# Folding two more modulation vectors onto 64 partitions in a linear-attention and token-mixer block

## The chip, the cores and the metric

The kernel runs on one core of a Trainium2 chip. The metric is device microseconds of one execution, median over runs. The engines are TensorE (PE, its weight loads as PEld), VectorE (DVE), ScalarE (ACT), GpSimd (POOL) and SyncE (SP, which issues most DMAs). Each executes its own instructions in program order, and they wait for each other by semaphores.

## The reference

With x of 2048 tokens by 448 channels (float32), 16 heads of 28 channels:

```python
mod = (silu(c) @ w_mod).reshape(1, 6, 1, 448)
sa, ca, ga, sb, cb, gb = mod[:, 0], ..., mod[:, 5]
h = layernorm(x) * (1 + ca) + sa
x = x + ga * linear_attention(h, wqkv, wo)      # phi(q) (phi(k)^T v) / (phi(q) sum phi(k))
h = layernorm(x) * (1 + cb) + sb
x = x + gb * token_mlp(layernorm(h), w1, b1, w2, b2)   # gelu MLP across the 2048 tokens
```

The six modulation vectors are numbered 0 to 5 here and in the code: 0 and 1 are sa and ca of the attention, 2 is ga, 3 is sb, 4 is cb (1 + cb is stored), 5 is gb. The change concerns vectors 3 and 4, the fourth and fifth.

## The kernel before

Tokens come in 16 tiles of 128. A value in float32 that TensorE is to multiply exactly is cut into a high part (rounded to TensorE's float32r) and a low part (the rest), and a product is taken as two or three float32r matmuls. The program is scheduled by hand: what an engine does, and in which order, is the order in which the code issues it.

**Modulation vectors 2 to 5.** The rows of w_mod for vector j come as four tiles `wm{j}_{k}` of 112 partitions. `mod_part(j, k)` multiplies tile k with silu(c) and adds it into `acc{j}` (112 x 448) on VectorE. Then `mod_split(j)` prepares `acc` for TensorE, and `mod_sum2(j)` sums over the partitions with a matmul whose weights are all ones, so that the sum stands on all 128 partitions; `mod_out` copies it out of PSUM on ScalarE. `mod_split` has two ways:

```python
    def mod_split(j):
        acc = macc.pop(j)
        if j in FOLDED:
            both, low = halves(acc, slot, f"mh{j}")
            low()
            macc[j] = (both,)
        else:
            macc[j] = (moving(slot, f"mh{j}", parts=G), moving(slot, f"ml{j}", parts=G))
            split(acc, *macc[j])
```

- Not folded: `split` (lines 84 and 85) makes the high part `mh` by a copy on ScalarE and the low part `ml` by a subtraction on VectorE, each 112 x 448 in a buffer of its own, and `mod_sum2` (line 260) issues two matmuls.
- Folded: `halves` adds partitions 64 to 111 of `acc` to partitions 0 to 47 (VectorE, line 238), copies the 64 partitions that remain to partitions 0 to 63 of one buffer on ScalarE (line 240: the high part), and `low` writes the difference to partitions 64 to 127 of the same buffer (VectorE, line 243). `mod_sum2` then issues one matmul over 128 partitions.

**Stage 1** is a loop over the tiles t = 4 to 15 (tiles 0 to 3 are begun ahead of it): project k, its exponential and relu, the normalized tokens `xn` cut into `xh` and `xl`, phi(k) cut into `pkh` and `pkl`, and their outer products, which add into four PSUM banks `cacc` (`a_outer`, line 551) four tiles later. Each tile ends with odd jobs: `mod_part` of vector 4 at t = 9 to 12 (by `MOD_AT`), of vector 3 at t = 13 and 14, `mod_split(2)` at t = 11, the multiplication of a tile of `wo` with vector 2 from t = 13, and loads of `pr`, pieces of w1, by SyncE (`load_to`, line 316). The exponentials of q for the next tile (`eq`, `rq`, lines 468 and 469) are issued at the start of the next tile.

**The tail of stage 1.** Behind the loop stand, in the order of issue: the last `pk` parts; the sum of all phi(k), cut into `zh` and `zl`; the outer products of tiles 12 to 15; the last `wo` and the last two `mod_part` of vector 3; `split_to(2)`, which cuts two pieces of w1 (`ph` on ScalarE, `pl` on VectorE); the `zp` matmuls and their copy `zb`; `mod_split(4)`, `mod_split(3)`; `split_to(4)`; two q projections; the four `cs` (line 795 on ScalarE, 796 on VectorE); `split_to(6)`; `mod_sum2(4)`; the `kvb` matmuls (line 805), which read `cs`; `mod_sum2(3)`. From `kvb` come `kvm`, the `wp` matmuls and the weights `Wph`, `Wpl` of the output projection.

**Stage 2** is a loop over the tiles for the output projection, the two layer norms (which use vectors 4 and 3) and the first MLP product; stage 3 is the rest of the MLP. Nothing in them is edited.

**Buffers.** Tiles of SBUF made with `slot` share a pool of 74 buffers. A tile takes a free one, and its first writer, be it an engine or a DMA, waits until the last reader of the buffer's former tile is done.

Of the kernel before, what the change touches and what calls it, by code (L numbers as in the profile page):

```python
# [41 lines left out]
WARM = 6  # L42
POOL_LOW = (0, 2)
PRE = 9
FOLDED = (2, 5,)
MID = 5
NSLOT, NTOK = 74, 27
LOAD2, SPLIT2 = 12, 4
# [4 lines left out]
def block_kernel(ctx: ExitStack, tc: tile.TileContext, x, xt, wqkv, wo, w1, b1, w2, b2, c, wmod, wfirst, out):  # L53
# [23 lines left out]
    def moving(new, name, dt=F32R, parts=P):  # L77
        return new(name, dt=dt, parts=parts, w=512)[:, 16:16 + D]
# [4 lines left out]
    def split(full, hi, lo):  # L83
        nc.scalar.activation(hi, full, AF.Copy)  # L84
        nc.vector.tensor_sub(lo, full, hi.bitcast(F32))  # L85
# [150 lines left out]
    def halves(acc, new, name):  # L236
        n = acc.shape[0] - 64
        nc.vector.tensor_add(acc[:n], acc[:n], acc[64:])
        both = moving(new, name)
        nc.scalar.activation(both[:64], acc[:64], AF.Copy)  # L240

        def low():
            nc.vector.tensor_sub(both[64:], acc[:64], both[:64].bitcast(F32))
        return both, low
# [11 lines that stand above are left out]
    def mod_sum2(j):  # L256
        ps = bank(f"modp{j}")
        part = macc.pop(j)
        for i, m in enumerate(part):
            nc.tensor.matmul(ps[:, :D], ones_r[:m.shape[0], :], m, start=(i == 0), stop=(i == len(part) - 1))  # L260
        return ps
# [11 lines left out]
    def w_low(j, ch):  # L273
        w, r = Whi[j, ch], raw_w[j, ch]
        p = slice(0, P) if ch < 3 else slice(64, P)
        if ch < 3:
            Wlo[j, ch] = moving(tslot, f"wl{j}_{ch}")
        out = Wlo[j, ch] if ch < 3 else w[p]
        nc.vector.scalar_tensor_tensor(out, r[p], col[1][p, ch:ch + 1], w[p].bitcast(F32),
                                       op0=ALU.mult, op1=ALU.subtract)  # L280

    def row_part(j, ch):
        if ch == 0:
            accb[j] = slot(f"accb{j}")
            nc.vector.tensor_scalar_mul(accb[j], raw_w[j, 0], col[0][:, 0:1])
        else:
            nc.vector.scalar_tensor_tensor(accb[j], raw_w[j, ch], col[0][:, ch:ch + 1], accb[j],
                                           op0=ALU.mult, op1=ALU.add)

    def row_sum(j):  # L290
        rowb[j] = bank(f"rowb{j}")
        ws = [Whi[j, ch] for ch in range(4)] + [Wlo[j, ch] for ch in range(3)]
        for i, w in enumerate(ws):
            nc.tensor.matmul(rowb[j][:ROWS, :D], sel_s, w, start=(i == 0), stop=False)

    def row_bias(j):
        nc.tensor.matmul(rowb[j][:ROWS, :D], sel_b, accb.pop(j), start=False, stop=True)
# [82 lines left out]
    def a_stats_dve(ts):  # L380
        g, ve = a_group(ts)

        b6 = {}

        def first(i):
            b6[i] = small.tile([P, 6], F32, name=f"st{ts[i]}", tag="st")
            nc.vector.bn_stats(b6[i], X[ts[i]])

        def second(i):
            nc.vector.bn_aggr(mv[ts[i]][:, 0:2], b6[i])  # L390

        def end():
            nc.vector.tensor_scalar_add(ve, g[:, :, 1:2].to_broadcast([P, len(ts), 2]), EPS)
            a_pow(g, ve)
            groups[ts[0]] = g
        return first, second, end
# [11 lines left out]
    def a_transpose(t):  # L408
        ps = bank(f"rw{t}")
        tps[t], tps[t + 1] = ps[:ROWS - 64, :P], ps[64:ROWS, :P]  # L410
        nc.tensor.transpose(ps[:ROWS, :P], rowst[t // 2 % RING][:, :ROWS].bitcast(F32), ident)
# [29 lines left out]
    def project(t, j, name):  # L441
        projects([(t, kind, ch) for ch in range(3) for kind in ("hh", "wl", "hl")] + [(t, "hh", 3)], j, name)

    def close(t, j):
        ps = pps.pop((t, j))
        nc.tensor.matmul(ps[:, :D], heads[t][1][:ROWS, 384:], Wrow[j][:ROWS], start=False, stop=True)  # L446
        return ps[:, :D]
# [31 lines left out]
    def a_q(t):  # L479
        project(t, 0, "qp")  # L480
        qps[t] = close(t, 0)
        del heads[t]
# [5 lines left out]
    def a_phi_q(keep=0):  # L488
        a_exp_q(keep)
        for t in sorted(eqs):  # L490
            pq[t] = phi_q(t)
# [50 lines left out]
    def a_outer(t):  # L542
        if not cacc:
            cacc.extend(bank(f"cacc{ch}") for ch in range(4))
        xh, xl = xss.pop(t)
        kh, kl = pks.pop(t)
        for ch in range(4):
            s = slice(ch * P, (ch + 1) * P)
            todo = [(xh, kh), (xh, kl)] + ([(xl, kh)] if ch < 3 else [])
            for i, (a, b) in enumerate(todo[::1 if t > 1 else 2]):  # L550
                nc.tensor.matmul(cacc[ch][:, :D], a[:, s], b, start=(t == 0 and i == 0),  # L551
                                 stop=(t == NT - 1 and i == len(todo) - 1))
        if t < 2:
            for ch in range(4):
                nc.tensor.matmul(cacc[ch][:, :D], xh[:, ch * P:(ch + 1) * P], kl, start=False, stop=False)
# [118 lines left out]
    for t in range(4, NT):  # L674
        if 5 < t < NT - 1:
            project(t + 1, 1, "kp")
        kp = close(t, 1) if t > 4 else kps[4]
        if t == 9:
            row_sum(0)
            row_bias(0)  # L680
        if t > 4:
            a_outer(t - KV_LAG)
        if t % 2 and 4 < t < NT - 2:
            a_transpose(t + 1)
        if t in Q_EARLY:
            a_q(Q_EARLY[t])
        if t == 12:
            mp = mod_sum2(2)
        pair = t % 2 and 7 < t + 3 < NT
        if pair:  # L690
            first, second, end = a_stats_dve((t + 3, t + 4))
            first(0)
        if 5 <= t < 9:
            w_low(0, t - 5)
        if pair:
            second(0)
        if 5 <= t < 9:
            row_part(0, t - 5)
        a_phi_q(t in Q_EARLY)
        if t == 9:  # L700
            a_exp(t, kp)
        if t % 2 and 4 < t < NT - 2:
            a_copy(t + 1)
            a_copy(t + 2)
        if t != 9:
            a_exp(t, kp)
        if 7 < t + 3 < NT:
            a_split_high(t + 3)
        a_pk_parts(t - 1)
        highs = HIGH_AT.get(t, (t - 2,))  # L710
        for i in highs[:1]:
            a_norm(i)
            a_high(i)
        if t % 2 == 0 and 4 < t < NT - 3:
            low = a_rows(t + 2)
        a_pk(t, kp)
        if t % 2 == 0 and 4 < t < NT - 3:
            low()
        if 7 < t + 3 < NT:
            a_split_low(t + 3)  # L720
        for i in highs[1:]:
            a_norm(i)
            a_high(i)
        if pair:
            first(1)
        for i in highs:
            a_low(i)
        if pair:
            second(1)
            end()  # L730
        sum_end()
        if 4 <= t < 8:
            w_high(0, t - 4)
            if t == 7:
                w_row(0)
        if t == 9:
            row_out(0)
        if t == 12:
            mod_out(2, mp)
            make_mask()  # L740
        if t in FETCH:
            load_xt(FETCH[t])
            load_x(FETCH[t])
        if 7 <= t < 11:
            mod_part(2, t - 7)
        if t == 11:
            mod_split(2)
        for j, i in MOD_AT.get(t, ()):
            mod_part(j, i)
        if t in (7, 10):  # L750
            load_mod(4 if t == 7 else 3)
        if t == 10:
            load_qkv(2, tslot)
        if t == 8:
            for g in range(4):
                w = tslot(f"wo{g}", parts=G)
                nc.sync.dma_start(w, wo[g * G:(g + 1) * G, :])
                wo_sb.append(w)
            b1c = cst.tile([P, NF], F32, name="b1c")
            nc.sync.dma_start(b1c, b1)  # L760
            b2c = cst.tile([P, NT], F32, name="b2c")
            nc.sync.dma_start(b2c, b2)
        if t >= 13:
            nc.vector.tensor_mul(wo_sb[t - 13], wo_sb[t - 13], mods[2][:G])
        load_to(PRE_LOAD.get(t, 0))
# [18 lines left out]
        nc.tensor.matmul(zp[:, :D], ones_r, pk, start=(i == 0), stop=(i == 1))  # L784
    zb = tslot("zb")
    nc.scalar.activation(zb, zp[:, :D], AF.Copy, bias=S * 1e-6)
    mod_split(4)
    mod_split(3)
    load_to(14)
    split_to(4)  # L790
# [184 lines left out]
    for i in range(NT + LAG):  # L975
# [15 lines left out]
        t = i - LAG  # L991
# [277 lines left out]
    for o0, n in W1G[1:]:  # L1269
# [5 lines left out]
        for r in range(first, NT):  # L1275
# [5 lines left out]
            if xleft:  # L1281
                t = xleft.pop(0)
# [81 lines left out]
```

## Time and profile before

| | |
|---|---|
| median of 3 runs | 436.17 us (435.62 to 436.36) |
| profiled execution | 435.4 us, span 433.7 us |
| PE busy | 428.1 us (99%), 2333 matmuls |
| DVE busy | 362.2 us (84%), 813 instructions |
| ACT busy | 278.5 us (64%), 595 instructions |
| POOL busy | 119.6 us (28%) |
| chain that ended last | PE 92%, DVE 4%, DMA 2% |

Times in the profile count from the start of the span, and lines (L260) are those of the kernel's code. A row of the timeline has the start, the duration, engine, line, operation, output and inputs by the program's names, shape and count; behind it, in brackets, how long the engine was idle just before and what it waited for. Rows that follow each other and are alike are merged ("x2"). Durations of pipelined instructions overlap, so that the distance from start to start, not the duration, is what an instruction costs its engine's queue.

### The profile page before, as it was taken

The numbers are of one execution on the slowest core, as the hardware profiler recorded it, in microseconds if no ns is written. First come the engines' busy times: TensorE is split into PE (matmuls) and PEld (weight loads), VectorE is DVE, ScalarE is ACT, GpSimd is POOL, SyncE is SP. The second block draws the span as 40 slices with busy tenths as digits, with TensorE's granted clock in tenths as the row PEclk, the third lists the DMA queues.
The fourth block names the chain that finished last, engine by engine and source line by source line (L and its number), as shares of the span: only waits on it lengthen the run. The fifth ranks groups of instructions, "written<-read, shape, count | busy, mean of one in ns | idle before, by whom it ended". The sixth has DMA issues, their size and how long they took to land.

```text
span 433.7 us, 7208 instructions
## 1 busy us (share of the span) xinstructions
PE 428.1 (99%) x2333; PEld 395.5 (91%) x2333; DVE 362.2 (84%) x813; ACT 278.5 (64%) x595; POOL 119.6 (28%) x198
## 2 busy tenths in 40 slices
PE   8999999999999999999999999999999999999996
PEld 7788899999899989989999999999999999999996
DVE  4999987689799999996579695739799998898893
ACT  5899868658578799985855263537464664645550
POOL 2336444300025577775200000010113131122010
PEclk9999999999999999999999999999999999999999
DMA  8998996574200036345427461587479977886430
GB/s 278 384 334 179 242 249 152 107 225 164 86 1 0 26 73 148 73 98 121 147 85 241 144 212 50 167 209 201 85 181 215 228 157 153 218 176 125 82 54 32
DMA packets 63941, 66.14 MB, mean 152 GB/s; under 512 B 4960, under 2 KB 55456, under 8 KB 63904
## 3 DMA queue, kind: packets, MB, share of 16 engines
q1 hardware_dynamic: 54832, 50.90, 37.8%
q0 software_dynamic: 8784, 14.32, 21.1%
q10 hardware_dynamic: 288, 0.46, 0.5%
q8 instruction: 18, 0.29, 0.3%
q14 instruction: 19, 0.16, 0.1%
HBM read 46.30 MB, written 7.34 MB: 124 GB/s over the span
## 4 chain that ended last, share of the span: by engine, by line
PE 92%; DVE 4%; DMA 2%; issue 0%; POOL 0%; ACT 0%; SPq 0%; DVEq 0%
PE y L1159 19%; PE up L939 10%; PE up L938 10%; PE up L940 10%; PE y L1160 9%; PE cacc L551 8%; PE qp L439 7%; PE op L881 6%; PE kp L439 5%; PE tq L851 1%; PE op L888 1%; DMA wr<-in_qkv_dram 1%; DMA xt<-in_xt_dram 1%; PE qp L446 1%; PE kvb L805 1%; PE wp L955 1%
## 5 line engine op out<-in xcount | busy, mean ns | idle before, releaser
L939 PE MATMUL up<-h2l,ph 128*128 128x448 f32 x224 | 81.3, 363 | 0.0
L938 PE MATMUL up<-h2h,ph 128*128 128x448 f32 x224 | 81.2, 362 | 0.0
L940 PE MATMUL up<-h2h,pl 128*128 128x448 f32 x224 | 80.8, 361 | 0.0
L1114 POOL DMA_DIRECT2D a<-a x16 | 14.2, 962 | 137.8 <-DMA a<-in_B_w_dram 77.6
L938 PEld LDWEIGHTS up<-h2h,ph 128*128 128x128 f32 x224 | 42.0, 188 | 3.2
L940 PEld LDWEIGHTS up<-h2h,pl 128*128 128x128 f32 x224 | 41.9, 187 | 3.0
L939 PEld LDWEIGHTS up<-h2l,ph 128*128 128x128 f32 x224 | 42.0, 188 | 2.6 <-DVE h2l L935 0.3
L85 DVE TENSOR_TENSOR pl<-pr,ph 128x512 fp32r<-128x512 f32 x46 | 30.8, 688 | 4.1 <-ACT ph L84 3.3
L1165 ACT ACTIVATE cc<-y 128x448 f32<-128x448 f32 x24 | 13.0, 546 | 26.8 <-PE y L1160 26.8
L84 ACT ACTIVATE ph<-pr 128x512 fp32r<-128x512 f32 x46 | 27.6, 623 | 0.8 <-PE up L940 0.5
L1078 DVE TENSOR_TENSOR u<-u,mod 128x448 f32<-128x448 f32 x14 | 8.7, 623 | 21.7 <-ACT u L1077 21.5
L1077 ACT ACTIVATE u<-up,b1c 128x448 f32<-128x448 f32 x14 | 8.8, 625 | 24.1 <-PE up L940 23.5
L1179 POOL DMA_DIRECT2D out_dram<-yt x14 | 12.7, 908 | 40.8 <-DVE yt L1170 31.4
L439 PE MATMUL kp<-wh,hh 128*128 128x448 f32 x64 | 23.7, 375 | 0.0
L551 PE MATMUL cacc<-pkh,xh 128*128 128x448 f32 x64 | 23.6, 369 | 0.0
L439 PE MATMUL qp<-wh,hh 128*128 128x448 f32 x64 | 23.4, 366 | 0.0
L831 POOL TENSOR_SCALAR den<-den 128x16 f32<-128x16 f32 x16 | 8.8, 549 | 45.4 <-DVE den L828 45.4
L551 PE MATMUL cacc<-pkl,xh 128*128 128x448 f32 x56 | 20.3, 362 | 0.0
L881 PE MATMUL op<-wph,pth 128*128 128x448 f32 x48 | 18.7, 390 | 0.0
L1120 DVE TENSOR_TENSOR a<-a,s 128x512 f32<-128x512 f32 (+1 forms) x32 | 18.5, 622 | 0.0
L84 ACT ACTIVATE s2h<-s 128x512 fp32r<-128x512 f32 (+1 forms) x16 | 8.3, 569 | 15.5 <-DVE s L1120 15.5
L1159 PE MATMUL y<-ub,a11h 128*128 128x448 f32 x56 | 18.2, 375 | 0.0
(239 smaller groups left out, 1378.1 us busy)
## 6 DMA issues: line engine op xcount, KB each, us to landing
pr<-in_B_w_dram SPq DMA_DIRECT2D x56, 256.0 KB, 3.1
a<-in_B_w_dram SPq DMA_DIRECT2D x32, 256.0 KB, 4.4
a<-in_B_w_dram SPq DMA_DIRECT2D x32, 192.0 KB, 4.2
xt<-in_xt_dram SPq DMA_DIRECT2D x16, 256.0 KB, 5.0
x<-in_A_x_dram SPq DMA_DIRECT2D x16, 224.0 KB, 5.0
wm<-in_B_wmod_dram SPq DMA_DIRECT2D x16, 196.0 KB, 5.4
out_dram<-x SPq DMA_DIRECT2D x14, 224.0 KB, 2.2
out_dram<-yt POOLq DMA_DIRECT2D x14, 224.0 KB, 5.7
```

The lines of the kernel that those rows point to most:

```text
L84: nc.scalar.activation(hi, full, AF.Copy)
L85: nc.vector.tensor_sub(lo, full, hi.bitcast(F32))
L439: nc.tensor.matmul(pps[t, j][:, :D], a[:, ch * P:(ch + 1) * P], w, start=first, stop=False)
L551: nc.tensor.matmul(cacc[ch][:, :D], a[:, s], b, start=(t == 0 and i == 0), stop=(t == NT - 1 and i == len(todo) - 1))
L881: nc.tensor.matmul(opb[t][:, :D], a, b, start=(ch == n == 0), stop=False)
L938: nc.tensor.matmul(ps[:, :D], hi[:, sl], mh, start=first, stop=False)
L939: nc.tensor.matmul(ps[:, :D], hi[:, sl], ml, start=False, stop=False)
L940: nc.tensor.matmul(ps[:, :D], lo[:, sl], mh, start=False, stop=last)
L1114: nc.gpsimd.dma_start(w, a, accum_op=ALU.add)
L1120: nc.vector.tensor_tensor(w, raw2[q, a][i], raw2[q, b][i], op=op)
L1159: nc.tensor.matmul(ps[:, :D], h[:, s], w, start=opens and r == 0, stop=False, skip_group_check=True)
L1160: nc.tensor.matmul(ps[:, :HD], l[:, s], wh, start=False, stop=closes and r == PAIRS - 1, skip_group_check=True)
```

## The change

Vectors 3 and 4 join 2 and 5 in `FOLDED`, so that `mod_split` takes the folded way for them and `mod_sum2` issues one matmul each. `mod_split(4)`, which stood behind the copy `zb` in the tail, is issued in the loop instead, at t = 14, ahead of that tile's `mod_part(3, 1)`. `mod_split(3)` stays in the tail.

```diff
-FOLDED = (2, 5,)
+FOLDED = (2, 3, 4, 5)
...
         if t == 11:
             mod_split(2)
+        if t == 14:
+            mod_split(4)
         for j, i in MOD_AT.get(t, ()):
             mod_part(j, i)
...
     nc.scalar.activation(zb, zp[:, :D], AF.Copy, bias=S * 1e-6)
-    mod_split(4)
     mod_split(3)
     load_to(14)
     split_to(4)
```

## Prediction

> **What bounds the kernel now.** I read the engine totals first, then the chain of work that ended last, then the waits of TensorE, and last the timeline of each engine around the two places where the diff edits. Totals and chain of the page:
>
> ```profile
> PE 428.1 (99%) x2333; PEld 395.5 (91%) x2333; DVE 362.2 (84%) x813; ACT 278.5 (64%) x595; POOL 119.6 (28%) x198
> ...
> PE 92%; DVE 4%; DMA 2%; issue 0%; POOL 0%; ACT 0%; SPq 0%; DVEq 0%
> ```
>
> TensorE is busy for 99% of the span and is 92% of the chain. It executes in program order and there is hardly an idle stretch behind its start, so a matmul that goes saves its time, and any stall that comes is paid in full: no later wait is large enough to take it back. The question is therefore only what VectorE (DVE) and ScalarE (ACT) hand to TensorE late. One stage of the windows view, and the one wait of a weight load in this region (waits of PEld):
>
> ```profile
> core 0: us, PE busy (x) PEld busy (x) DVE busy (x) ACT busy (x) POOL busy (x), PEclk, DMA share, GB/s
> 97.80:102.80 5.00, 5.00 (x26) 4.52 (x25) 4.96 (x10) 4.58 (x10) 0.00 (x0) 1.00 0.53 188
> PEld kvb L805 <- DVE cs L796: 0.2, 1, 0.2
> ```
>
> From 97.8 to 102.8 us VectorE is busy for 4.96 of 5.00 us, and what stands at the end of that stretch, the four `cs` operations, is what the `kvb` matmuls wait for. TensorE reaches `kvb` just as the first `cs` ends: cover there is zero, though TensorE loses nothing yet. TensorE in that region, from its timeline:
>
> ```profile
> 93.62 0.36 PE L551 MATMUL cacc<-pkh,xl 128*128 128x448 f32 x1
> ...
> 97.82 0.36 PE L784 MATMUL zp<-zl,ones_r 128*128 128x448 f32 x1
> ...
> 102.43 0.36 PE L260 MATMUL modp<-mh,ones_r 112*128 112x448 f32 x1
> 102.64 0.37 PE L260 MATMUL modp<-ml,ones_r 112*128 112x448 f32 x1
> 102.84 3.40 PE L805 MATMUL kvb<-cs,wr 128*112 128x112 f32 x32
> ...
> 106.29 0.36 PE L260 MATMUL modp<-ml,ones_r 112*128 112x448 f32 x1
> ```
>
> The reader is to see the starts, not the durations: 448-column matmuls overlap and start every 0.20 us (102.43, 102.64, 102.84).
>
> **The change, part by part.**
>
> *One matmul instead of two, twice.* The `ml` matmuls of vectors 3 and 4 go. Each is one start interval, 0.20 us: 0.40 us off TensorE, 0.09% of the time. The one of vector 4 stands right ahead of `kvb`, so its 0.20 us counts only if `kvb` doesn't wait; the one of vector 3 stands behind `kvb` and counts in any case.
>
> *What a fold costs VectorE and ScalarE.* The kernel already folds vector 2 at the end of tile 11, with the same code in the same order. VectorE, then ScalarE, from their timelines:
>
> ```profile
> 68.84 0.17 DVE L393 TENSOR_SCALAR ve<-mv 128x4 f32<-128x4 f32 x1
> 69.04 0.62 DVE L238 TENSOR_TENSOR acc<-acc 48x448 f32<-48x448 f32 x1
> 70.30 0.62 DVE L243 TENSOR_TENSOR mh<-acc,mh 64x448 fp32r<-64x448 f32 x1 [0.65 <-ACT mh L240]
> 70.95 0.69 DVE L233 SCALAR_TENSOR_TENSOR acc<-wm,sc,acc 112x448 f32<-112x448 f32 x1
> 69.69 0.58 ACT L240 ACTIVATE mh<-acc 64x448 fp32r<-64x448 f32 x1 [1.71 <-DVE acc L238]
> 70.18 0.61 ACT L468 ACTIVATE eq<-qp,mv 128x448 f32<-128x448 f32 x1
> ```
>
> A fold is add, copy, subtract, each waiting for the one before on the other engine. Add to copy takes 0.65 us (69.04 to 69.69), copy to subtract 0.61, subtract to the next VectorE operation 0.65: 1.91 us of VectorE's queue for 1.24 us of work. Half the partitions save nothing, 0.62 us being also what 112 rows take (the `ml` row below, two in 1.16). ScalarE stands behind its copy: 1.71 us idle for it. At tile 11 both had room. In these rows the add starts 0.03 us behind the end of `ve` (68.84 + 0.17), and the operation behind the subtract 0.03 us behind its end, while unlike the rows below (0.53 to 0.60 us from start to start of 0.62 to 0.68 us operations) they don't overlap; I take 0.03 us.
>
> [...]
>
> *The fifth vector's split at tile 14.* It now stands behind the low parts of tile 13 and ahead of the multiply-add of vector 3 on VectorE, and on ScalarE behind the copy `xh` and ahead of `eq` of tile 15. ScalarE and VectorE there, before:
>
> ```profile
> 85.71 0.58 ACT L503 ACTIVATE xh<-xn 128x448 fp32r<-128x448 f32 x1 [1.65 <-DVE xn L499]
> 86.61 0.64 ACT L468 ACTIVATE eq<-qp,mv 128x448 f32<-128x448 f32 x1 [0.31 <-PE qp L446]
> ...
> 88.69 0.59 ACT L519 ACTIVATE pkh<-pk 128x448 fp32r<-128x448 f32 x1
> 86.47 0.55 DVE L509 TENSOR_TENSOR xl<-xn,xh 128x384 fp32r<-128x384 f32 x1
> 86.93 0.68 DVE L233 SCALAR_TENSOR_TENSOR acc<-wm,sc,acc 112x448 f32<-112x448 f32 x1
> 87.53 0.62 DVE L764 TENSOR_TENSOR wo<-wo,mod 112x448 f32<-112x448 f32 x1
> 88.06 0.62 DVE L473 SCALAR_TENSOR_TENSOR pq<-eq,rq 128x448 f32<-128x448 f32 x1
> 89.31 0.63 DVE L521 SCALAR_TENSOR_TENSOR pkl<-pk,pkh 128x448 fp32r<-128x448 f32 x1 [0.63 <-ACT pkh L519]
> ...
> 91.91 0.55 DVE L509 TENSOR_TENSOR xl<-xn,xh 128x384 fp32r<-128x384 f32 x1
> ...
> 96.23 0.62 DVE L85 TENSOR_TENSOR zl<-pk,zh 128x448 fp32r<-128x448 f32 x1 [0.70 <-ACT zh L84]
> ```
>
> The add starts when `xl` is done, 86.47 + 0.55 + 0.03 = 87.05; the copy 0.65 later at 87.70; `eq` 0.49 behind that (69.69 to 70.18) at 88.19 instead of 86.61: ScalarE is 1.58 us late. `pkh` goes from 88.69 to 90.27 and ends at 90.86. VectorE: subtract at 88.31, multiply-add at 88.96 (2.03 us late), `pq` by the old distances at 90.09, done at 90.71, so `pkl` still waits for `pkh` and starts at 90.89: 1.58 us late. Behind it the two engines only wait for each other (`xn` to `xh`, sum to `zh` to `zl`), so I carry 1.58 us on to `zl`: 97.81. Of the idle 0.63 and 0.70 us nothing is gained, since the engine that causes each idle stretch is as late. The bounds: 0.25 us, if both idle stretches do absorb (1.58 - 1.33), and 2.03 us, if VectorE's own delay decides.
>
> What waits for it on TensorE: the low part of tile 14 (the `xl` of 91.91) ends at 94.04 instead of 92.46. Its matmul starts at 93.62, and its weights load one interval of 0.20 us ahead; so TensorE stalls some 0.6 us, and at `zl` (97.82 before) perhaps 0.2 us more. Neither enters the sum: `kvb` will wait longer, and swallows them.
>
> *The tail.* Behind `zl` VectorE did, before:
>
> ```profile
> 98.63 1.29 DVE L85 TENSOR_TENSOR pl<-pr,ph 128x512 fp32r<-128x512 f32 x2
> 99.83 1.16 DVE L85 TENSOR_TENSOR ml<-acc,mh 112x448 fp32r<-112x448 f32 x2
> 100.90 1.29 DVE L85 TENSOR_TENSOR pl<-pr,ph 128x512 fp32r<-128x512 f32 x2
> 102.10 2.47 DVE L796 SCALAR_TENSOR_TENSOR cs<-zb,col,cs 128x448 f32<-128x448 f32 x4
> ```
>
> The two `ml` subtracts (99.83 to 100.90, 1.07 us) go; add and subtract of vector 3 come, as many operations as went, but with the round trip over ScalarE between them, for which VectorE has nothing else in its queue. `pl` starts at 98.63 + 1.58 = 100.21, the pair ends 1.29 later at 101.50; add 101.53, copy 102.18 (ScalarE has only `zb` ahead of it and is free), subtract 102.79, the next `pl` pair 103.44, and `cs` 1.20 us behind (100.90 to 102.10) at 104.64 instead of 102.10. So 2.54 us late, of which 0.96 us is the tail's. Bounds of that 0.96: 0.13 us with no idle time between (1.20 against 1.07), 0.96 with all of it. I take 0.96, the walk by the nearest fold.
>
> `kvb` starts at 102.84 + 2.54 = 105.38. Without the wait TensorE would be there about 2 us earlier. Behind `kvb`, the `ml` matmul of vector 3 is saved. Sum: 2.54 - 0.20 = +2.34 us.
>
> *Edits at nothing.* The fold takes one buffer of the pool for the two of `mh` and `ml`, and vector 4 takes its one earlier; in return its accumulator is free earlier. Those that queue for buffers are SyncE's loads of `pr`:
>
> ```profile
> 82.75 23.19 SPq L316 DMA_DIRECT2D pr<-in_B_w_dram  x17
> 96.11 1.14 ACT L84 ACTIVATE ph<-pr 128x512 fp32r<-128x512 f32 x2
> ```
>
> The split issues no DMA on SyncE or on GpSimd. The first loads go out at 82.75, their user starts at 96.11; one buffer's turn later costs nothing under 13 us of cover. If it were gone, a split of `pr` would wait for a load. The opposite shift behind the tail (two buffers fewer) can only bring loads forward.
>
> **The time.** The sum stands against the profiled execution, 435.4 us with a span of 433.7: 437.7. The median of the runs shown is 436.17, 0.8 us above the profiled one, so as a median 436.17 + 2.34 = 438.5 us.
>
> **The rivals.** A difference under 0.2%, 0.87 us, can hardly be told from none here (the runs shown already spread from 435.62 to 436.36).
>
> First, that it is not slower: ScalarE's idle stretches hide the round trips, so that `cs` comes no later than before, and the two matmuls are the whole effect: 436.17 - 0.40 = 435.8. For it speak ScalarE's idle stretches (1.71 us at the fold of vector 2, 1.65 us ahead of `xh` at 85.71). Against it: VectorE is full from 97.8 on, `kvb` has no cover, and the copy stands in front of `eq` in a queue that runs in order. It decides at once: every tenth of a us by which `cs` is late beyond 0.20 eats into the gain.
>
> Second, half the price: VectorE's idle 0.63 and 0.70 us take up most of the fold at tile 14, because `pkl` or `zl` is not held by ScalarE as I think; then 0.25 + 0.96 - 0.20 = +1.0, 437.2 us.
>
> Third, more: VectorE's 2.03 us instead of 1.58 carry through, and TensorE's freed matmul doesn't show because the first transpose behind the `wp` matmuls waits for a `pn` as late as `cs`: 2.03 + 0.96 = +3.0 us, 439.2; a late load of `pr` on top would make it about 439.7.
>
> **How the numbers follow.** The sum above 0.70, with a range of its own from 437.9 to 439.1 (0.2 to 0.3 us for each hand-over and the spread of the runs); the first rival 0.10, the second 0.12, the third 0.08. The range from 436.9 to 439.6 takes in the second and the third and leaves out the first. Slower by over 0.2%: 0.70 + 0.08 + half the second, whose +1.0 us is close to the bound, 0.84; within 0.2%: the other half and most of the first, 0.13; faster by more, for which the two matmuls alone don't suffice, 0.03.
>
> **What would show it.** In the profile after: `kvb` waiting near 2 us for `cs`, which starts near 104.6; `eq` of tile 15 near 88.2, with `mh` in front of it; a VectorE idle time of about 0.65 us before each L243; the matmul of tile 14's `xl` stalled by some 0.6 us; `modp` with four 128-row matmuls and none of 112 rows. I am wrong if `cs` starts within 0.5 us of 102.1, or if TensorE takes the delay back behind `kvb`, which needs idle time of TensorE in the old trace that I did not see.

## The result, and the profile after

The changed kernel takes 438.31 us (median of 5 runs, 437.71 to 439.63); the kernel before, run beside it, 435.62 us (435.16 to 436.36). The ratio is 1.0061, interval 1.0040 to 1.0082: 2.7 us slower, where +2.3 us was forecast. The forecast median, 438.5 us, is off by 0.2 us only, which is in part luck: it stood on 436.17 us for the kernel before, 0.55 us above this median, while the effect was 0.35 us larger than forecast. The profiled execution took 438.38 us with a span of 436.7.

The page after, totals and chain:

```profile
PE 429.4 (98%) x2331; PEld 397.3 (91%) x2331; DVE 363.9 (83%) x815; ACT 278.5 (64%) x595; POOL 119.5 (27%) x198
...
PE 87%; DMA 6%; DVE 4%; ACT 1%; issue 1%; POOL 0%; SPq 0%; DVEq 0%
```

Two matmuls fewer, two VectorE instructions more, and a chain that leaves TensorE more often. Where the time went is read from TensorE's timeline. Profiled executions reach the same instruction up to 0.9 us apart (the `kp` matmul below stands at 86.40 to 87.28 us in all the kernels), so I measure from a fixed place: the **gauge** is the time from the last `kp` matmul of tile 15 to the first `tq` matmul. Before:

```profile
86.41 0.37 PE L446 MATMUL kp<-wrow,hl 98*128 98x448 f32 x1
...
111.70 0.49 PE L851 MATMUL tq<-ident,pn 128*128 128x128 f32 x3
```

and after:

```profile
86.88 0.37 PE L446 MATMUL kp<-wrow,hl 98*128 98x448 f32 x1
...
94.55 0.47 PE L551 MATMUL cacc<-pkh,xl 128*128 128x448 f32 x1 [0.27 <-DVE xl L509]
...
103.67 0.37 PE L260 MATMUL modp<-mh,ones_r 128*128 128x448 f32 x1
105.88 3.40 PE L806 MATMUL kvb<-cs,wr 128*112 128x112 f32 x32 [1.83 <-DVE cs L797]
109.05 0.45 PE L260 MATMUL modp<-mh,ones_r 128*128 128x448 f32 x1
...
114.68 0.52 PE L852 MATMUL tq<-ident,pn 128*128 128x128 f32 x3
```

The gauge goes from 25.30 to 27.79 us (unrounded starts): +2.49. From the first `tq` to the last matmul both executions take 318.5 us, equal within 0.01 us. So the loss lies in these 28 us (the 0.48 us by which the changed execution reaches the `kp` matmul later is within the 0.9 us just named), and the biggest piece of it is the bracket behind `kvb`: 1.83 us of TensorE waiting for `cs`, where there was none. What made `cs` late, VectorE, then two rows of ScalarE, after:

```profile
86.95 0.55 DVE L509 TENSOR_TENSOR xl<-xn,xh 128x384 fp32r<-128x384 f32 x1
87.53 0.62 DVE L238 TENSOR_TENSOR acc<-acc 48x448 f32<-48x448 f32 x1
88.80 0.62 DVE L243 TENSOR_TENSOR mh<-acc,mh 64x448 fp32r<-64x448 f32 x1 [0.64 <-ACT mh L240]
89.45 0.69 DVE L233 SCALAR_TENSOR_TENSOR acc<-wm,sc,acc 112x448 f32<-112x448 f32 x1
...
91.34 0.63 DVE L521 SCALAR_TENSOR_TENSOR pkl<-pk,pkh 128x448 fp32r<-128x448 f32 x1
...
98.25 0.62 DVE L85 TENSOR_TENSOR zl<-pk,zh 128x448 fp32r<-128x448 f32 x1 [0.70 <-ACT zh L84]
...
100.64 1.29 DVE L85 TENSOR_TENSOR pl<-pr,ph 128x512 fp32r<-128x512 f32 x2
101.96 0.62 DVE L238 TENSOR_TENSOR acc<-acc 48x448 f32<-48x448 f32 x1
103.29 0.62 DVE L243 TENSOR_TENSOR mh<-acc,mh 64x448 fp32r<-64x448 f32 x1 [0.70 <-ACT mh L240]
103.94 1.29 DVE L85 TENSOR_TENSOR pl<-pr,ph 128x512 fp32r<-128x512 f32 x2
105.15 2.47 DVE L797 SCALAR_TENSOR_TENSOR cs<-zb,col,cs 128x448 f32<-128x448 f32 x4
...
113.91 0.62 DVE L839 SCALAR_TENSOR_TENSOR pn<-pq,den 128x448 f32<-128x448 f32 x1
88.19 0.58 ACT L240 ACTIVATE mh<-acc 64x448 fp32r<-64x448 f32 x1 [1.41 <-DMA pr<-in_B_w_dram]
88.67 0.61 ACT L468 ACTIVATE eq<-qp,mv 128x448 f32<-128x448 f32 x1
```

Both folds show: a subtract 1.3 us behind its add, with VectorE idle 0.64 and 0.70 us for the copy between. The copy's bracket names a DMA; but the add ends at 87.53 + 0.62 = 88.15 and the copy starts 0.04 us later, so it was the add (in the traces of two kernels below, the one with an extra copy and the changed one with filling, the same idle 1.41 us is put down to `acc`, the add). This is how a wait on several semaphores misleads: check the named releaser against the other candidates' ends.

### The profile page after: what moved, and what is told of

Same layout as the page of the kernel before. It is cut to its first block, busy times and chain, and to the rows that moved or that the text cites. A ratio compares the mean times of both kernels' runs of the same rounds, so it can differ in the third digit from the quotient of the medians.

```text
span 436.7 us, 7206 instructions
## 1 busy us (share of the span) xinstructions
PE 429.4 (98%) x2331; PEld 397.3 (91%) x2331; DVE 363.9 (83%) x815; ACT 278.5 (64%) x595; POOL 119.5 (27%) x198
## 4 chain that ended last, share of the span: by engine, by line
PE 87%; DMA 6%; DVE 4%; ACT 1%; issue 1%; POOL 0%; SPq 0%; DVEq 0%
PE y L1160 19%; PE up L940 10%; PE up L939 10%; PE up L941 10%; PE y L1161 9%; PE qp L439 6%; PE op L882 6%; PE cacc L551 6%; PE kp L439 5%; DMA xt<-in_xt_dram 2%; DMA wr<-in_qkv_dram 2%; PE tq L852 1%; PE op L889 1%; DMA pk<-pk 1%; PE kvb L806 1%; PE wp L956 1%
```

## The experiments

All distances below are from the `kp` matmul of the gauge (the anchor), in us, out of each kernel's profiled execution. Times are medians, ratios against the kernel before on the same chip (its medians beside the experiments were 435.42 to 435.73 us).

| kernel | eq | zl | cs | kvb | pn | tq = gauge | time | ratio (interval) |
|---|---|---|---|---|---|---|---|---|
| before | 0.20 | 9.83 | 15.70 | 16.43 | 24.20 | 25.30 | | |
| changed | 1.79 | 11.36 | 18.26 | 19.00 | 27.02 | 27.79 | 438.31 | 1.0061 (1.0040 to 1.0082) |
| fold 3 only, in the tail | 0.20 | 9.82 | 17.20 | 17.93 | 25.96 | 26.73 | 437.11 | 1.0030 (1.0018 to 1.0042) |
| fold 4 only, at tile 14 | 1.79 | 11.37 | 16.71 | 17.44 | 25.21 | 26.32 | 436.61 | 1.0022 (1.0013 to 1.0031) |
| move only, no fold | 0.26 | 9.88 | 15.22 | 16.43 | 23.71 | 25.22 | 435.48 | 0.9996 (0.9986 to 1.0005) |
| both folds in the tail | 0.20 | 9.82 | 18.68 | 19.41 | 29.54 | 30.99 | 441.28 | 1.0117 (1.0091 to 1.0144) |
| changed, cs first | 1.79 | 11.36 | 17.05 | 17.79 | 27.01 | 27.78 | 438.30 | 1.0063 (1.0048 to 1.0079) |
| changed, extra copy | 2.44 | 12.03 | 18.93 | 19.66 | 28.49 | 29.95 | 439.50 | 1.0089 (1.0074 to 1.0105) |
| folds spread | 0.20 | 9.82 | 16.23 | 16.97 | 24.73 | 25.64 | 435.96 | 1.0009 (1.0000 to 1.0018) |
| folds spread, cs and pn first | 0.20 | 9.82 | 15.02 | 16.23 | 23.52 | 24.84 | 435.42 | 0.9994 (0.9985 to 1.0002) |
| both in the tail, TensorE filled | 0.20 | 9.82 | 18.68 | 19.41 | 27.43 | 28.20 | 438.49 | 1.0068 (1.0053 to 1.0083) |
| changed, TensorE filled | 1.79 | 11.36 | 18.27 | 19.00 | 27.03 | 27.80 | 438.22 | 1.0062 (1.0045 to 1.0079) |

**One part at a time.** Fold 3 only:

```diff
-FOLDED = (2, 5,)
+FOLDED = (2, 3, 5)
```

> Gauge: time from the start of the last kp matmul of stage 1 (L446, tile 15) to the first tq matmul; before 25.30 us, changed kernel 27.79. Theory (each round trip add, copy, subtract holds VectorE, which has no cover ahead of kvb): the unfolded split of vector 4 stays in the tail, so the fold of vector 3 replaces one subtract (0.53 us) by 2.02 us of queue; cs 1.5 us late, less 0.20 for one matmul: gauge 26.6 to 26.7, about +1.3 us. Rival (more VectorE work alone, one extra add of 0.6 us, waits hidden): gauge 25.5 to 25.7. Rival (the fold costs nothing, only the early place does): gauge 25.1.

Gauge 26.73, +1.43, at the upper end of the expectation (26.6 to 26.7): the round trip in the tail by itself costs `cs` 1.50 us. An extra add without waits (0.6 us) would not do it. VectorE in the tail of this kernel:

```profile
100.89 0.62 DVE L238 TENSOR_TENSOR acc<-acc 48x448 f32<-48x448 f32 x1
102.16 0.62 DVE L243 TENSOR_TENSOR mh<-acc,mh 64x448 fp32r<-64x448 f32 x1 [0.65 <-ACT mh L240]
```

Fold 4 only, at tile 14 (from the changed kernel):

```diff
-FOLDED = (2, 3, 4, 5)
+FOLDED = (2, 4, 5)
```

> Vector 4 folded at tile 14, vector 3 not folded, its split in the tail. Theory: ScalarE's eq is 1.58 us late, carried to zl; the tail is lighter by one subtract of 0.53 us; cs 1.05 us late, and no matmul saved behind kvb: gauge 26.3 to 26.5. Rival (VectorE's idle 0.63 and 0.70 us absorb the fold in the loop): gauge 25.1 to 25.3.

Gauge 26.32, +1.02, and `eq` and `zl` as late as in the changed kernel. VectorE's idle stretches absorb next to nothing (0.05 of 1.59 us). The two folds add up: +1.43 and +1.02 are +2.45, against +2.49 together.

The move alone (from the changed kernel):

```diff
-FOLDED = (2, 3, 4, 5)
+FOLDED = (2, 5)
```

> No folds beyond before, but the unfolded split of vector 4 is issued at tile 14. Its copy needs nothing late, as acc4 is finished at tile 12. Theory: copy runs in ScalarE's idle time before eq, eq some 0.1 us late, cs earlier by about 0.45 us, which TensorE doesn't need: gauge 25.2 to 25.35, time as before. Rival (the place itself costs, by work put ahead of eq or by other buffers): gauge above 25.9.

Gauge 25.22. ScalarE at tile 14, in this kernel:

```profile
86.28 0.56 ACT L84 ACTIVATE mh<-acc 112x448 fp32r<-112x448 f32 x1
86.75 0.63 ACT L468 ACTIVATE eq<-qp,mv 128x448 f32<-128x448 f32 x1
```

A copy at the same place in the queue (here of 112 rows) delays `eq` by 0.06 us (0.26 against 0.20), because it waits for nothing. So neither the place, nor the buffers that shift with it, costs anything in this kernel; what costs is the add that the copy must wait for.

Both folds at the old place (from the kernel before):

```diff
-FOLDED = (2, 5,)
+FOLDED = (2, 3, 4, 5)
```

> Both folded, both splits in the tail at their old place. Theory: nothing late up to zl (start 9.8 us behind the anchor as before); two round trips in VectorE's full queue, 3.9 us for 1.07: cs 2.9 us late, less 0.20, plus 0.1 to 0.2 for pn: gauge 27.9 to 28.2, slower than the changed kernel by 0.2 to 0.3 us. Rival (the move to tile 14 is what costs): gauge about 26.2.

`cs` is 2.98 us late, as expected, but the gauge is 30.99, three us past the expectation. Between `kvb` and `wp` lie 8.58 us instead of the 5.67 of the changed kernel. `cs` was as late as expected, so VectorE doesn't explain it; the two runs with filling below take it up.

**What the late VectorE holds up.** In the changed kernel, the w1 pieces ahead of `cs` go behind them:

```diff
-    split_to(4)
     a_q(late.pop(0))
...
         (the four cs)
+    split_to(4)
     a_phi_q()
```

> The changed kernel, with the two w1 splits (two ph, two pl) that stood ahead of the four cs issued behind them. cs comes 1.20 us earlier on VectorE. If the wait of kvb for cs is all the loss: gauge 27.79 - 1.2 = 26.6. If the loss is VectorE's backlog, which also holds pn: pn is as late as in the changed kernel, tq waits for it, gauge 27.6 to 27.8 and only the place of the stall moves, from kvb to tq.

The second reading holds: `kvb` is 1.21 us earlier, the gauge is 27.78, as before the edit. The stall moved along TensorE, here its timeline in this kernel:

```profile
104.24 3.40 PE L806 MATMUL kvb<-cs,wr 128*112 128x112 f32 x32 [0.66 <-DVE cs L796]
...
110.51 3.23 PE L956 MATMUL wp<-wo,kvm 112*112 112x448 f32 x8 [0.45 <-ACT ph L84]
114.23 0.52 PE L852 MATMUL tq<-ident,pn 128*128 128x128 f32 x3 [0.49 <-DVE pn L839]
```

Three small stalls in place of one large one. The bracket at `wp` names `ph`, which `wp` doesn't read; `kvm`, which it does read, ends on VectorE at 110.37, 0.14 us ahead of it. VectorE's backlog is what TensorE pays, and moving work from ahead of `cs` to ahead of `kvm` and `pn` only chooses where. To move it behind the first `pn` was not tried in the changed kernel; with spread folds it is, below.

One more copy ahead of `eq` in the changed kernel:

```diff
         if t == 14:
             mod_split(4)
+            nc.scalar.activation(junk[:64], macc[4][0][:64].bitcast(F32), AF.Copy)
```

> The changed kernel with one more ScalarE copy of 64 x 448 (into a scratch buffer) right behind the copy of the fold at tile 14, ahead of eq. Theory (ScalarE's lateness at eq carries through to cs and pn one to one): 0.47 to 0.5 us more, gauge 28.2 to 28.3. Rival (VectorE's idle times absorb lateness of ScalarE): gauge 27.8.

`eq` moves by 0.65 us (the copy reads the other's result, so it also waits for its end), `zl` by 0.67, `cs` by 0.67, `kvb` by 0.66: one to one, nothing absorbed. But the gauge is 29.95, where 28.2 to 28.3 was expected: behind `kvb` another 1.50 us is lost in this execution, in which the granted clock fell to 0.50 there (last section).

**Folds without waits.** Vector 4 is folded at the start of tile 13, in the idle stretch of both engines there; of vector 3, the add is issued right behind the last multiply-add and the rest where the split was:

```diff
+        if t == 13:                     # behind a_phi_q, instead of t == 14
+            mod_split(4)
...
         mod_part(3, i)
+    mod_add(3)                          # the add of halves
     split_to(2)
...
-    mod_split(3)
+    mod_halves(3)                       # copy and subtract
```

> Both vectors folded, but the waits given other work: vector 4 is folded at the start of tile 13, where both engines are idle; of vector 3 the add follows the last multiply-add, and copy and subtract stand where the split was, with two pl between add and subtract. Theory: eq and zl as before; VectorE's queue from the last multiply-add to cs is one add and one subtract for two ml, cs 0.35 us late; with 0.20 saved: gauge 25.4 to 25.6. Rival (the folds' work, not the waits, costs): gauge above 26.5.

Gauge 25.64, just past the range (25.4 to 25.6): `cs` is 0.53 us late instead of 0.35, VectorE in the tail of this kernel:

```profile
98.73 0.62 DVE L248 TENSOR_TENSOR acc<-acc 48x448 f32<-48x448 f32 x1
99.44 1.29 DVE L85 TENSOR_TENSOR pl<-pr,ph 128x512 fp32r<-128x512 f32 x2
100.77 0.62 DVE L254 TENSOR_TENSOR mh<-acc,mh 64x448 fp32r<-64x448 f32 x1
101.42 1.29 DVE L85 TENSOR_TENSOR pl<-pr,ph 128x512 fp32r<-128x512 f32 x2
```

No idle bracket at the subtract any more. But the add still takes 0.71 us to the next start and the subtract 0.65, where the `ml` took 0.53: 0.29 us of the 0.53. The other 0.24 are overlap that the neighbours lose: `pl`, or here the add, starts 0.11 us later behind the multiply-adds, and the `pl` pair takes 1.33 us to the next start instead of 1.20. The folds as such, then, are nearly free; 0.34 us of the 2.49 remain.

The same, with the w1 pieces ahead of `cs` behind them (`split_to(4)`) and those behind `kvm` behind the first `pn` (`split_to(8)`):

```diff
-    split_to(4)
     a_q(late.pop(0))
...
         (the four cs)
+    split_to(4)
...
-    split_to(8)
...
         (the first den and pn)
+    split_to(8)
```

> As the kernel before, with the two splits of w1 ahead of cs issued behind cs, and the two behind kvm issued behind the first pn. Theory: cs and pn no longer decide, TensorE runs through, both saved matmuls count: gauge 24.9, 0.4 us under the kernel before, which is less than the times can tell. Rival (pn, kvm or the later w1 pieces become the wait): gauge 25.3 or more.

Gauge 24.84, 0.46 us under the kernel before: both saved matmuls (0.40), and 0.10 at `kvb`, whose matmuls take 3.07 us to the next start (103.43 to 106.50) instead of the 3.17 before, where the first one's weight load waited 0.2 us for `cs`. From `wp` to `tq` nothing is gained (3.04 us, before 3.01). TensorE in this kernel:

```profile
103.22 0.37 PE L271 MATMUL modp<-mh,ones_r 128*128 128x448 f32 x1
103.43 3.31 PE L818 MATMUL kvb<-cs,wr 128*112 128x112 f32 x32
106.50 0.45 PE L271 MATMUL modp<-mh,ones_r 128*128 128x448 f32 x1
```

The gain stands in the trace and is too small for the times (0.9994, 0.9985 to 1.0002).

**The missing 3 us.** Both splits in the tail, again, and ahead of `kvb` 12 matmuls that nobody reads, in columns 448 to 511 of a PSUM bank:

```diff
     mp = mod_sum2(4)
+    for _ in range(12):
+        nc.tensor.matmul(mp[:, D:], ones, ones[:, :64], start=True, stop=True, skip_group_check=True)
     kvb = bank("kvb")
```

> The kernel with both splits in the tail (gauge 30.99 against 27.9 to 28.2 expected; granted clock 0.50 from 105.9 to 112.7 us, behind TensorE's idle 3.02 us at kvb), with 12 matmuls of 64 columns that nobody reads put ahead of kvb, into that idle time. If the idle time lowered the clock, and the clock stretched the kvb matmuls (6.32 us for 3.40): clock 1.00 throughout, cs and kvb start as before the filling, gauge 27.9 to 28.3, three us faster though TensorE has more to do. Rival (kvb is paced by cs, pn or something else in that stage): gauge stays near 31.

`cs` and `kvb` start where they did, the gauge falls from 30.99 to 28.20, the median from 441.28 to 438.49. (The 12 matmuls stand as 24 in the trace.) First `kvb` and the windows row of 105.90 to 112.60 without the filling (busy times by engine, then the granted clock, share and GB/s of DMA):

```profile
106.53 6.32 PE L805 MATMUL kvb<-cs,wr 128*112 128x112 f32 x32 [3.02 <-DVE cs L796]
105.90:112.60 6.70, 6.07 (x33) 6.07 (x33) 4.72 (x8) 5.71 (x12) 0.00 (x0) 0.50 0.38 117
```

then with it:

```profile
103.51 2.79 PE L802 MATMUL modp<-ones 128*128 128x64 f32 x24
106.69 3.40 PE L807 MATMUL kvb<-cs,wr 128*112 128x112 f32 x32 [0.40 <-DVE cs L796]
105.90:112.60 6.70, 6.30 (x49) 5.94 (x49) 6.50 (x12) 5.87 (x12) 0.00 (x0) 1.00 0.40 117
```

Granted clock 0.50 against 1.00, `kvb` 6.32 us against 3.40. The idle time of 3.02 us had a second price here: the granted clock fell to 0.50, and 2.79 us more were lost behind it.

The changed kernel with 8 such matmuls:

```diff
     mp = mod_sum2(4)
+    for _ in range(8):                  # as above
```

> The changed kernel with 8 such matmuls ahead of kvb (its idle time there is 1.83 us). They are hidden by the wait for cs: gauge 27.7 to 27.9, time as the changed kernel's undisturbed executions, 437.7 to 438.4, and no execution with a granted clock of 0.996 or less, of which the changed kernel had one in five (439.63 us). Rival (the filler delays kvb): gauge above 28.0.

Gauge 27.80, granted clock 0.999 to 1.000, times of 437.95 to 438.75 in four executions, one of them (438.75) above the 437.7 to 438.4 expected. It agrees in the main, and shows little: the changed kernel without filling had one lowered clock in five.

## Why the prediction was right, point by point

- *The two matmuls, 0.40 us.* As said: the one behind `kvb` counts (`kvb` +2.57, `wp` 22.29 to 24.67, +2.38), the one ahead of it not, since `kvb` waits.
- *The fold at tile 14, ScalarE 1.58 us late.* `eq` 1.79 behind the anchor instead of 0.20: 1.59. `zl` 1.53 to 1.54 late, against 1.58. Fold 4 alone, the move alone and the extra copy show the chain link by link: the copy waits for the add, `eq` for the copy, and what follows up to `kvb` for `eq`.
- *VectorE's 1.91 us for a fold's 1.24 us of work.* After: 87.53 to 89.45 is 1.92. The add starts 0.03 us behind `xl`'s end (86.95 + 0.55), the operation behind the subtract 0.03 behind its end. Rows near them overlap (in the same trace the multiplication of `wo`, 0.62 us long, starts at 90.05 and the next row at 90.58, 0.53 behind). What keeps these two from it, no run shows.
- *The tail, 0.96 us more.* 2.56 us late at `cs` less 1.53 at `zl` is 1.03. The second copy cost 0.70 us of VectorE's idle time, not 0.65.
- *TensorE's small stalls do not add.* 0.57 us of stall by the first `zp` (11.21 to 11.78) and 0.06 more by the second, forecast as 0.6 and 0.2; `kvb` swallowed them.
- *No cost for buffers.* The move alone, which takes two buffers earlier, shows none: 25.22.
- *Sum +2.34, gauge +2.49.* Of the missing 0.15, 0.03 is `kvb` (2.57 late, not 2.54). The other 0.12 is the piece that I put into the third rival alone: `pn` is 2.82 us late and `tq` waits for it (in five of the kernels, this one among them, `tq` starts 0.77 us behind the start of `pn`; before it was 1.10), so that more than half of the matmul saved behind `kvb` is lost again. It belonged into the sum. The medians differ by 2.69; the median of the four executions without a lowered clock (the fifth has 439.63 us, clock 0.996) is 438.17, 2.55 more than before.
- *The rivals.* Absorption by idle time (first and second) fell with fold 4 alone and the extra copy. Of the third, VectorE's own 2.03 us did not carry through (`zl` 1.53 late), while the late `pn` did count, with 0.12 us.

What I left out: the granted clock of TensorE. In the changed kernel, whose profiled execution idled 1.83 us at `kvb`, one execution of five has a lower mean clock (0.996, the others 0.999 to 1.000); in the kernel with both folds in the tail, whose profiled execution idled 3.02 us, all four have (0.992 to 0.994).

## What to carry to other kernels

Count a step that hands data to another engine and back as the sum of the durations, not as its work: here three operations of 0.6 us cost VectorE's queue 1.9 us, and the queue of the other engine as well (1.59 us at `eq`), where the copy stands ahead of urgent work. Before saving a matmul this way, ask whether the engines that prepare it have idle time there; put the three steps apart, with other work of the queue between: here the same two folds then cost 0.34 us of the gauge instead of 2.49. And where an engine's backlog is the loss, moving its first customer forward only moved the stall to the next (gauge 27.78 against 27.79); in the kernel with spread folds the stall went (gauge 24.84 instead of 25.64) when the w1 pieces went behind `cs` and `pn`.

## What the runs showed of the hardware

**The granted clock fell to 0.50 in a trace with 1.86 us of idle time, and not in one with 1.83.** In the kernel with the extra copy TensorE idled 1.86 us at `kvb`, 0.03 more than in the changed kernel. In its profiled execution, `kvb` and the windows around it:

```profile
106.15 5.01 PE L807 MATMUL kvb<-cs,wr 128*112 128x112 f32 x32 [1.86 <-DVE cs L798]
103.40:106.80 3.40, 1.54 (x11) 1.14 (x10) 3.21 (x6) 3.40 (x8) 0.00 (x0) 1.00 0.10 17
106.90:110.20 3.30, 3.30 (x20) 3.30 (x20) 3.13 (x6) 3.30 (x8) 0.00 (x0) 0.50 0.59 163
110.40:116.00 5.60, 5.60 (x27) 4.10 (x26) 4.27 (x9) 2.01 (x5) 0.29 (x1) 1.00 0.06 25
```

Its four executions fall into two groups: 438.85 and 438.86 us at a mean clock of 0.999, 440.14 (the profiled one) and 440.27 at 0.996. So about 1.4 us go with the lowered clock. By these rows the stretch at 0.50 lasts 3.3 to 3.6 us and begins 0.65 to 0.75 us after TensorE is busy again. In the kernel with both folds in the tail it lasts 6.7 to 7.0 us, and begins 0.6 to 0.7 us ahead of `kvb` (106.53), while TensorE is still idle:

```profile
102.00:105.80 3.80, 1.51 (x8) 1.07 (x6) 3.04 (x6) 2.47 (x5) 0.00 (x0) 1.00 0.02 5
105.90:112.60 6.70, 6.07 (x33) 6.07 (x33) 4.72 (x8) 5.71 (x12) 0.00 (x0) 0.50 0.38 117
112.80:119.00 6.20, 6.20 (x27) 4.37 (x26) 5.02 (x9) 2.32 (x5) 0.56 (x2) 1.00 0.12 37
```

In the changed kernel's trace, with 1.83 us of idle time at the same place, the clock stands at 1.00 from 90 to 118 us; with fold 3 alone and 1.3 us the mean clock is 1.000. Why the clock fell in one trace and not in the other, and in two of four executions of one kernel, no run shows.

**A VectorE subtraction took longer beside GpSimd work.** In the two kernels with spread folds the subtract at tile 13 took 1.10 us (77.85 to 78.95 in the first), while GpSimd wrote the mask (76.68 to 78.48); the subtract of every other fold took 0.62. The add of the same fold took its usual 0.62 beside that GpSimd work (76.58 to 77.20). Whether the one slowed the other was not tried.
